# Turning the first eight attention units in four 64x64 tiles of TensorE, with diagonal blocks made by GpSimd

## The chip, the cores and the metric

The kernel runs on one core of one Trainium2 chip. The metric is the device time of one execution in microseconds. The core has five engines that run side by side, each through its own list of instructions in order: TensorE (PE in the profile; its weight loads are shown as PEld), VectorE (DVE), ScalarE (ACT), GpSimd (POOL), and SyncE (SP), which issues nearly all DMA transfers. They wait for each other through semaphores.

## What is computed

Two layers follow each other. The first is an attention in which only scores near the maximum of their row count; the second is a bilinear feed-forward layer. Cut from the reference:

```
q, k, v: (8, 8, 576, 64) float32; w_a, w_b: (512, 1536), w_out: (1536, 512) float64
scores = (q @ k^T) / sqrt(64)
thresh = max(scores, -1) - tau                       # tau = 0.02
attn   = exp(where(scores >= thresh, scores, -1e9) - max(scores, -1))
attn   = attn / (sum(attn, -1) + 1e-9)
x      = (attn @ v), heads side by side               # (4608, 512)
out    = ((x @ w_a) * (x @ w_b)) @ w_out              # (4608, 512) float32
```

## The kernel before

**Units.** Heads are taken in pairs (`i`, 32 of them), and the 576 query rows of a pair in blocks of 128 (`u`). A unit `(i, u)` is one such block for both heads of a pair, and the program is one long loop over the units (line 1062); I call one pass of it a slot. A unit goes through a pipeline that stretches over several slots, and PE's matmuls of the second layer are put between the steps of the first by `advance`, which counts matmul columns against a planned pace.

**The steps of a unit.** In slot `g`: `scores` (lines 389 to 413) makes the scores of both heads in PSUM (line 404) and takes the row maxima on DVE (line 411) and the thresholds (line 412). `weigh` (422 to 438) takes the exponential on ACT (lines 431 and 432), and on DVE masks it and sums the rows (line 435). `reciprocal` (440 to 449) makes `rcp`, one over each row's sum, on DVE. To multiply the weights by v, they have to be turned, so that the 576 keys lie on partitions. There are two ways for that:

- From the ninth unit on, `normalise` multiplies by `rcp` on ACT (line 454), and the blocks are turned on DVE (line 498) and through DRAM.
- The first eight units (`BY_PE = 8`: the first two blocks of the first four head pairs) are turned by PE. `diagonals` (456 to 463) makes, on ACT, a 128x128 identity times `rcp` for each of the two heads (line 462). In the next slot `turn_pe` (468 to 482) multiplies the weights by that diagonal: for each of nine groups of 64 keys and each head one matmul with 128 rows, 64 columns of weights and 128 moving columns (line 479). So the turn normalises as well. The results lie in two PSUM tiles: `tp` for the first eight groups, four to a bank, and `last` for the ninth. ACT copies `tp` to SBUF in two halves (line 481), DVE copies `last` (line 482).

One slot later still, `weighted_unit` (590 to 604) multiplies the turned weights by v (`product`, line 542: 36 matmuls in four 64x64 tiles of the array), `settle` copies the product out of PSUM (ACT line 549, DVE line 550), and `exchange` (line 565) copies halves across partitions on GpSimd. A float32 matmul stands in the trace as two records, each with a load of its own.

**Beside it: the weights of the second layer.** They are float64 in DRAM and are converted on the chip in 36 pieces of 128x512, two or three to a slot in the first slots. SP loads them (line 271, each tied to a PE instruction that was written before it, so that loads don't run ahead of the work). ACT takes the high and low words (lines 298 and 299), GpSimd clamps (line 305), DVE moves in the sign and shifts (lines 311 and 319), GpSimd adds (line 324). The order within a slot is written out in the loop: the remaining conversion steps of the pieces of the slot before are spread over it (`convert_rest`, lines 1092, 1146 and 1149), and the new pieces begin at lines 1138 and 1150. `diagonals` stands at line 1142: behind the clamp of the slot's first piece, ahead of the add of the earlier slot's second piece.

**PSUM** is handed out in four tiles of two banks (`banks`), shared by scores, turns, products and the second layer. Once a tile's reader is done, another takes it.

`make_identity` fills `ident` at line 350 on GpSimd. The diagonals lie in the space behind the turned q of the first four pairs (`first_sb`), in three places used in turn.

Of the kernel before, what the change touches and what calls it, by code (L numbers as in the profile page):

```python
# [13 lines left out]
AF = mybir.ActivationFunctionType  # L14
ALU = mybir.AluOpType
# [39 lines left out]
def kernel(  # L55
# [38 lines left out]
    nc = tc.nc  # L94
    B, H, S, D = q.shape
    P = 128
# [3 lines left out]
    HP = H // 2  # L100
    NT = 4
# [26 lines left out]
    def banks(n, name):  # L128

        return psum.tile([P, 2, 512], FP32, tag="banks", name=name)[:, :, 0:n]  # L130
# [95 lines left out]
    for f in range(NG):  # L226
        for c in range(HP):
            for dst, w in ((wa_sb, w_a), (wb_sb, w_b)):
                src = []
                for r in range(2):  # L230
                    chunks = [(2 * c + e) % HP * 2 + (r + (c >= HP // 2)) % 2 for e in range(2)]
                    cols = slice(f * CW + r * CH, f * CW + (r + 1) * CH)
                    rows = w[:, cols].bitcast(U32).rearrange("(k p) f -> p k f", p=D)
# [16 lines left out]
    first_sb = first_u32.bitcast(FP32)  # L250
# [97 lines left out]
    load_rows(3, "k", rooms[7])  # L348
    ident = more_sb[:, 2 * QUARTER:2 * QUARTER + P]
    make_identity(nc, ident)  # L350

# [14 lines left out]
    def prep_pe(i, name):  # L368

        m = loaded[i][name]  # L370
        if name == "q":
            mT = first_sb[:, i * S:(i + 1) * S]
        else:
            mT = work.tile([P, S], FP32, tag="kT", bufs=HP, name="kT")
        tp = banks(SH, "tp")
        for c in range(2):
            for n in range(NR // 2):
                nc.tensor.transpose(tp[:, c, n * R:(n + 1) * R], m[:, c * (NR // 2) + n], ident[0:R, 0:R])
        prepared.setdefault(i, {})[name] = mT
        return mT, tp  # L380
# [75 lines left out]
    def diagonals(i, u):  # L456

        ws, rcp = weights[i, u]
        g = units.index((i, u))
        dg = first_sb[:, HP * S + g % 3 * 2 * P:HP * S + (g % 3 + 1) * 2 * P].rearrange("p (j q) -> p j q", j=2)  # L460
        for j in range(2):
            nc.scalar.activation(dg[:, j], ident, AF.Copy, scale=rcp[:, j:j + 1])
        weights[i, u] = (ws, dg)

    def turned_tile():
        return work.tile([P, G + 1, NSLOT, Q], FP32, tag="wT", bufs=2, name="wT")

    def turn_pe(i, u):

        ws, dg = weights.pop((i, u))  # L470
        ws = [w.rearrange("p n e -> p (n e)") for w in ws]
        wT = turned_tile()[:, 0:G].rearrange("p g s e -> p (g s e)").rearrange("p (s w) -> p s w", w=P)
        turned[i, u, "pe"] = [wT[:, :, y * D:(y + 1) * D] for y in range(2)]
        tp = banks(512, "tp").rearrange("p y (s q) -> p y s q", s=NT)
        last = banks(P, "tp")
        for s in range(NSLOT):
            for j, w in enumerate(ws):
                to = (last[:, 0] if s == 2 * NT else tp[:, s // NT, s % NT])[j * D:(j + 1) * D]
                nc.tensor.matmul(to, w[:, s * D:(s + 1) * D], dg[:, j], start=True, stop=True)  # L479
        for y in range(2):  # L480
            nc.scalar.copy(wT[:, y * NT:(y + 1) * NT], tp[:, y])
        nc.vector.tensor_copy(wT[:, 2 * NT], last[:, 0])

    def parts(i, u):

# [553 lines left out]
    kT, tp = prep_pe(0, "k")  # L1039
# [22 lines left out]
    for g in range(len(units) + PV_LAG):  # L1062
# [49 lines left out]
        if 0 < g <= BY_PE:  # L1112
            turn_pe(*units[g - 1])
# [27 lines left out]
        if here and g < BY_PE:  # L1141
            diagonals(i, u)
        elif here:
            reciprocal(i, u, nc.scalar if converting else nc.vector)
            normalise(i, u)
# [80 lines left out]
```

## Time and profile before

| what | value |
|---|---|
| runs | 1420.72 us median of 3 (1419.43 to 1420.96) |
| profiled execution, first to last instruction (span) | 1417.0 us |
| median of the runs less that span | 3.7 us |
| mean granted clock of TensorE | 0.994 |
| busy over the span: PE / DVE / ACT / POOL | 1370.2 / 1013.7 / 679.9 / 495.7 us |
| records of line 479 (turn) | 288 matmuls, first at 19.0, last at 80.5 us, mean 0.30 us each as shown |
| records of line 462 (diagonals) | 16 on ACT, 0.41 us each as shown |
| line 481 / line 482 (copies of the turn) | 16 on ACT at 0.59 us / 8 on DVE at 0.27 us |
| PE idle before line 479 | 3.3 us "issue", 2.9 ACT, 0.6 ACT, 0.5 DVE (PE and PEld together) |
| busy in the stretch 0 to 100 us, line 479 on PE | 20.6 us |

The execution's own timed value is not given beside its profile, so its span stands for it. Matmuls are pipelined: the time shown for one is longer than the distance to the next, so a run of 36 records is measured from its first start to its last end. In the timeline one row merges neighbouring instructions of one line: start, length, engine, line, what it writes and reads, how many, and in brackets the idle time before it with what ended it.

### The profile page before, as it was taken

Reading aid. Unit: us, or ns where it says so; the run is one execution under the profiler, and the core shown is the slowest. Engines: PE = TensorE matmul, PEld = TensorE weight load, DVE = VectorE, ACT = ScalarE, POOL = GpSimd, SP = SyncE. Lnnn points to the kernel's source line nnn. Section 1 sums busy time; section 2 is a strip of 40 time slices with the busy share of each in tenths; the row PEclk is TensorE's granted clock in tenths of the full one; section 3 lists DMA queues with packets and bytes.
Section 4 is the critical chain, followed back from the end, with each engine's and each line's share of the span. In section 5 each row is a group of like instructions: output and inputs, shape, how many; then the busy total and the mean of one; then the engine's idle time right before and its main releaser. Section 6 shows DMA issues by size and latency. Waiting matters only on the chain.

```text
span 1417.0 us, 76257 instructions
## 1 busy us (share of the span) xinstructions
PE 1370.2 (97%) x33836; PEld 1229.6 (87%) x33836; DVE 1013.7 (72%) x2200; ACT 679.9 (48%) x1245; POOL 495.7 (35%) x678
## 2 busy tenths in 40 slices
PE   6788999999999999999999999999999999999998
PEld 5677579989878887979998999999888899799997
DVE  6898986778777877776767777677777776744424
ACT  5786554545445454545444545454545455431110
POOL 2674541606060606042333324150606060608100
PEclk9999999999999999999999999999999999999999
DMA  9967776667756775666555675567655775550000
GB/s 212 235 193 219 182 214 163 178 153 183 198 135 173 198 188 155 178 156 184 142 134 149 168 193 158 144 160 199 168 144 152 191 201 154 135 152 18 4 19 18
DMA packets 327000, 223.20 MB, mean 158 GB/s; under 512 B 171536, under 2 KB 310800, under 8 KB 326672
## 3 DMA queue, kind: packets, MB, share of 16 engines
q1 hardware_dynamic: 323712, 216.95, 59.2%
q8 instruction: 266, 4.36, 1.3%
q10 hardware_dynamic: 2960, 1.38, 0.4%
q14 instruction: 62, 0.51, 0.1%
HBM read 128.58 MB, written 89.65 MB: 154 GB/s over the span
## 4 chain that ended last, share of the span: by engine, by line
PE 86%; DVE 7%; DMA 3%; issue 2%; SPq 1%; ACT 0%; POOL 0%; DVEq 0%; POOLq 0%; ACTq 0%
PE pab L720 29%; PE po L885 20%; PE pab L824 16%; PE pv L542 10%; PE sc L404 10%; DVE mx L411 2%; DVE tw L498 2%; SPq L144 1%; DMA wT<-swap 1%; DVE tw L435 1%; PE tp L479 1%; DMA raw<-in_moe_w_a_dram 1%; DMA raw<-in_moe_w_b_dram 1%; DVE thr L412 0%; DVE u L790 0%
## 5 line engine op out<-in xcount | busy, mean ns | idle before, releaser
L411 DVE TENSOR_REDUCE mx<-sc 128x1 f32<-128x576 f32 x288 | 204.7, 752 | 125.8 <-PE sc L404 125.4
L454 ACT ACTIVATE tw<-tw,rcp 128x576 f32<-128x576 f32 x272 | 196.5, 770 | 202.3 <-DVE rcp L448 202.3
L682 POOL TENSOR_TENSOR h<-h,u 128x512 f32<-128x512 f32 x28 | 35.2, 1276 | 601.0 <-DVE h L794 426.1
L432 ACT ACTIVATE tw<-sc,bias,scalars 128x576 f32<-128x576 f32 x288 | 239.8, 833 | 10.9 <-PE pab L720 0.4
L435 DVE SCALAR_TENSOR_TENSOR tw<-sc,thr,tw 128x576 f32<-128x576 f32 x288 | 221.5, 799 | 10.4 <-ACT tw L432 9.9
L885 PE MATMUL po<-wo_sb,h 64*64 64x256 f32 x3264 | 205.8, 376 | 1.2 <-DVE h L794 1.1
L498 DVE STREAM_TRANSPOSE tw<-tw 128x576 f32<-128x576 f32 x272 | 194.4, 752 | 0.8 <-ACT tw L454 0.8
L885 PEld LDWEIGHTS po<-wo_sb,h 64*64 64x64 f32 x3264 | 157.0, 133 | 25.7 <-DVE h L794 2.6
L542 PE MATMUL pv<-wT,vm 64*64 64x160 f32 (+3 forms) x5184 | 169.2, 275 | 7.6 <-issue 3.6
L542 PEld LDWEIGHTS pv<-wT,vm 64*64 64x64 f32 x5184 | 157.4, 136 | 19.1 <-issue 9.8
L404 PE MATMUL sc<-kT,qT 64*64 64x288 f32 x2016 | 168.0, 404 | 1.1 <-DVE xt L550 0.5
L853 POOL TENSOR_TENSOR h<-h 128x256 f32<-128x256 f32 x168 | 117.4, 732 | 107.4 <-PE po L885 97.2
L885 PE MATMUL po<-sums_u,h 64*64 64x256 f32 x2448 | 153.4, 376 | 0.7 <-DVE h L832 0.7
L720 PE MATMUL pab<-xU,wb_sb 64*64 64x128 f32 x4352 | 138.0, 269 | 0.4 <-issue 0.3
L720 PEld LDWEIGHTS pab<-xU,wb_sb 64*64 64x64 f32 x4352 | 132.2, 133 | 3.7 <-issue 1.1
L885 PEld LDWEIGHTS po<-sums_u,h 64*64 64x64 f32 x2448 | 117.6, 133 | 19.4 <-DVE h L832 1.3
L404 PEld LDWEIGHTS sc<-kT,qT 64*64 64x64 f32 x2016 | 101.8, 133 | 22.6 <-issue 5.0
L549 ACT COPY xT<-pv 128x128 f32<-128x128 f32 (+1 forms) x68 | 17.7, 260 | 201.8 <-PE pv L542 200.2
L431 ACT ACTIVATE bias<-mx,scalars 128x1 f32<-128x1 f32 x288 | 83.1, 288 | 64.0 <-DVE mx L411 63.7
L550 DVE COPY xT<-pv 64x128 f32<-64x128 f32 (+1 forms) x136 | 38.1, 280 | 91.0 <-PE pv L542 89.7
L720 PE MATMUL pab<-xS,wa_sb 64*64 64x128 f32 x2176 | 101.8, 269 | 0.1
L531 ACT COPY kept<-po 128x512 f32<-128x512 f32 x65 | 34.8, 536 | 123.0 <-PE po L885 113.9
(156 smaller groups left out, 2414.3 us busy)
## 6 DMA issues: line engine op xcount, KB each, us to landing
wT<-swap SPq DMA_DIRECT2D x244, 288.0 KB, 3.9
swap<-tw SPq DMA_DIRECT2D x480, 144.0 KB, 2.9
vm<-in_v_dram SPq DMA_DIRECT2D x128, 72.0 KB, 2.5
swap<-tw SPq DMA_DIRECT2D x128, 72.0 KB, 3.0
kT<-in_k_dram SPq DMA_DIRECT2D x112, 72.0 KB, 3.3
wT<-swap SPq DMA_DIRECT2D x56, 144.0 KB, 3.3
out_dram<-kept SPq DMA_DIRECT2D x28, 256.0 KB, 3.9
qT<-in_q_dram SPq DMA_DIRECT2D x112, 40.0 KB, 2.8
```

The lines of the kernel that those rows point to most:

```text
L404: nc.tensor.matmul(sc[m][o * D:o * D + wide, c], qT[r, q0:q0 + wide], kT[r, c * SH:(c + 1) * SH], start=True, stop=True)
L411: nc.vector.tensor_reduce(mx[:, c], sc[j], axis=AX.XY, op=ALU.max)
L431: nc.scalar.activation(bias[:, j:j + 1], mx[:, j:j + 1], AF.Copy, scale=e_nscale)
L432: nc.scalar.activation(wb[j], sb[j], AF.Exp, bias=bias[:, j:j + 1], scale=e_scale)
L435: nc.vector.scalar_tensor_tensor(out=wv, in0=sb[j], scalar=thr[:, j:j + 1], in1=wv, op0=ALU.is_ge, op1=ALU.mult, accum_out=sums[:, j:j + 1])
L454: nc.scalar.activation(w, w, AF.Copy, scale=rcp[:, j:j + 1])
L498: nc.vector.transpose(w, w)
L542: nc.tensor.matmul(pv[c * D:(c + 1) * D, y], vm[rows, s], wT[y](rows, s), start=(s == 0), stop=(s == NSLOT - 1))
L720: nc.tensor.matmul(out[c * D:(c + 1) * D, r, f * P:(f + 1) * P], w[g][k][rows, w0:w0 + D], moving[k][rows], start=(fresh and k == 0 and f ...
L824: nc.tensor.matmul(pab[c:c + columns(), r], w[rows, f // n, k, fs + c:fs + c + columns()], moving, start=(k == 0), stop=(k == H - 1))
L853: (nc.vector if state["over"] else nc.gpsimd).tensor_tensor(*a, **kw)
L885: nc.tensor.matmul(po[c * D:(c + 1) * D, r, y], ht[rows, t0:t0 + D], other[rows, f], start=(f == 0), stop=(f == NF // 2 - 1))
```

## The change

The first eight units are turned in four tiles of 64x64 instead of two of 128x64. The 128 query rows of a unit fall in two halves of 64 (`r`). The diagonal matrix has nothing outside its two diagonal 64x64 blocks, so each half of the rows is multiplied only by its own block. Each matmul of 128 rows and 128 moving columns becomes two of 64 rows and 64 moving columns, and 18 matmuls to a turn become 36. Half `r` is written to bank `r` of the PSUM tile, so the copies to SBUF now take a half of the query rows each, with 64 of every 128 columns of the target.

The two diagonal blocks of both heads make a tile of 128x128 in place of two of 128x128. GpSimd makes it with one multiplication: `twice`, made once, holds the identity's two diagonal blocks on top of each other (64 columns), and is multiplied with `rcp` along the columns. ACT makes no diagonals any more. Order, tiles in PSUM, and everything behind the eighth unit's turn stay.

```diff
     make_identity(nc, ident)
+    twice = first_sb[:, HP * S + 3 * P:HP * S + 3 * P + D]
+    nc.gpsimd.tensor_tensor(twice, ident[:, 0:D], ident[:, D:P], op=ALU.add)
...
         ws, rcp = weights[i, u]
         g = units.index((i, u))
-        dg = first_sb[:, HP * S + g % 3 * 2 * P:HP * S + (g % 3 + 1) * 2 * P].rearrange("p (j q) -> p j q", j=2)
-        for j in range(2):
-            nc.scalar.activation(dg[:, j], ident, AF.Copy, scale=rcp[:, j:j + 1])
+        dg = first_sb[:, HP * S + g % 3 * P:HP * S + (g % 3 + 1) * P].rearrange("p (j q) -> p j q", j=2)
+        nc.gpsimd.tensor_tensor(dg, twice.unsqueeze(1).to_broadcast([P, 2, D]), rcp.unsqueeze(2).to_broadcast([P, 2, D]), op=ALU.mult)
         weights[i, u] = (ws, dg)
...
-        tp = banks(512, "tp").rearrange("p y (s q) -> p y s q", s=NT)
-        last = banks(P, "tp")
+        tp = banks(512, "tp").rearrange("p y (s q) -> p y s q", q=D)
+        last = banks(D, "tp")
         for s in range(NSLOT):
-            for j, w in enumerate(ws):
-                to = (last[:, 0] if s == 2 * NT else tp[:, s // NT, s % NT])[j * D:(j + 1) * D]
-                nc.tensor.matmul(to, w[:, s * D:(s + 1) * D], dg[:, j], start=True, stop=True)
-        for y in range(2):
-            nc.scalar.copy(wT[:, y * NT:(y + 1) * NT], tp[:, y])
-        nc.vector.tensor_copy(wT[:, 2 * NT], last[:, 0])
+            for r in range(2):
+                rows = slice(r * D, (r + 1) * D)
+                for j, w in enumerate(ws):
+                    to = (last[:, r] if s == 2 * NT else tp[:, r, s])[j * D:(j + 1) * D]
+                    nc.tensor.matmul(to, w[rows, s * D:(s + 1) * D], dg[rows, j], start=True, stop=True)
+        for r in range(2):
+            nc.scalar.copy(wT[:, 0:2 * NT, r * D:(r + 1) * D], tp[:, r])
+        nc.vector.tensor_copy(wT[:, 2 * NT].rearrange("p (r q) -> p r q", r=2), last)
```

## The prediction

> **What bounds the kernel now.** I read the head of the page first, because it says in which part of the span the change lies. The 288 matmul records of line 479, which are all that `turn_pe` issues, lie between 19.0 and 80.8 us of a span of 1417.0 us. So only the first 6% is touched, and what is gained or lost there has to be carried through to the end.
>
> ```profile
> span 1417.0 us, 76257 instructions
> ...
> PE   6788999999999999999999999999999999999998
> ...
> DMA  9967776667756775666555675567655775550000
> ...
> q8 instruction: 266, 4.36, 1.3%
> ```
>
> Each digit is a slice of 35.4 us. From the fifth slice on PE is busy nine tenths or more: whatever time PE has won or lost by then stays. In the first two slices it is only at six and seven tenths, so something else sets the pace there. The busy times by stretch name the candidate:
>
> ```profile
> core 0: us, PE busy (x) PEld busy (x) DVE busy (x) ACT busy (x) POOL busy (x), PEclk, DMA share, GB/s
> ...
> 20.00:44.00 24.00, 18.52 (x396) 15.16 (x392) 22.61 (x55) 20.29 (x44) 14.21 (x19) 1.00 1.17 223
> 44.00:70.00 26.00, 20.21 (x402) 17.57 (x403) 22.25 (x49) 19.36 (x40) 18.58 (x21) 0.93 1.05 237
> 70.00:100.00 30.00, 26.89 (x498) 24.10 (x499) 28.08 (x59) 26.23 (x53) 21.79 (x25) 0.94 0.66 187
> ```
>
> VectorE (DVE) is busy 22.61 of 24, 22.25 of 26 and 28.08 of 30 us, more than any other engine. In its timeline the row maxima of one step of the loop ("slot") follow those of the last at 25.34, 33.29, 39.90, 46.93, 56.82, 67.00, 77.71, 86.33 and 96.46 us, and between 33.3 and 77.7 it idles only 0.21, 0.47, 0.75, 0.93, 1.43 and 1.00 us: **4.8 us**. All six fall at or behind 49 us and wait for PE. So a faster PE can gain about 4.8 us here and no more, as long as DVE's own work stays.
>
> Why PE is late there, its timeline shows. The last bracket is the idle time before a row:
>
> ```profile
> 56.82 1.28 PE L542 MATMUL pv<-wT,vm 64*64 64x64 f32 x72
> 59.52 1.93 PE L479 MATMUL tp<-first_u,tw 128*64 128x128 f32 x31 [1.42 <-ACT tw L432]
> 62.58 0.54 PE L479 MATMUL tp<-first_u,tw 128*64 128x128 f32 x5 [1.13 <-issue]
> ...
> 70.09 0.34 PE L542 MATMUL pv<-wT,vm 64*64 64x64 f32 x6 [1.83 <-issue]
> 70.36 3.23 PE L479 MATMUL tp<-first_u,tw 128*64 128x128 f32 x36
> ```
>
> Two things are to be seen: the turn takes 2.2 to 3.2 us where 72 matmuls of 64x64 take 1.28, and PE waits for "issue", that is for nothing that the view can name. There are four such waits: 0.56 us until 47.29, 0.56 until 54.66, 1.13 until 62.58 and 1.83 until 70.09. I held them against the packets of queue q8 in the trace. Queue q8 carries 266 packets (4.36 MB) for PE's 67,672 matmuls and loads: 254 instructions to a packet. Its packets end at 45.72, 53.17, 61.09 and 68.63 us, and PE goes on 1.57, 1.49, 1.49 and 1.46 us later, each time exactly 256 instructions after the last stop. **PE waits there for its own instructions.** A packet starts 4.6 to 5.2 us after PE has entered the block before it, while the DMA share is over 1, and 1.1 to 1.9 us after it once the share has fallen to 0.66: about 7.5 us from block to block in the first case and 4.4 in the second.
>
> **The change part by part.** (1) *Turns on PE.* Now: 36 records a turn, 2.71, 2.19, 2.19, 2.48, 3.02, 2.47, 3.23 and 2.47 us, 20.8 in all. Afterwards: 9 slots x 2 halves x 2 heads x 2 records = 72 records of 64 columns through 64x64 tiles, the form of line 542's matmuls, hence 1.28 us each, 10.2 in all. Bounds: 1.2 us from the pv's own start-to-start, and 2.6 (no gain) from line 479 itself if the four tiles don't overlap. I take 1.28: PE loses **10.5 us** of work, of which only DVE's idle time can become time: **-4.8 us** at best. Zero is the other end. Were DVE not the cover, the whole 10.5 would count.
>
> (2) *Instructions for PE.* A turn has 72 loads and matmuls now and 144 after. A slot without the second layer goes from 232 to 304, one with three groups of 16 matmuls of line 824 from 328 to 400. At 7.5 us for 256 instructions, 400 would need 11.7 us where slots last 7 to 10.7. Moving the stops (every 256 instructions from the 449th) along the longer stream puts them in the pv of the fourth slot, the pv of the fifth, and the turn of the sixth, with waits of about 2.1, 3.2 and 4.2 us, and one of 0.8 in the eighth: 10.3 against 4.1 now. I let the packet's delay shrink as PE falls back, since line 271's loads are tied to PE's progress (SP's waits name PE sc, tp and pab): a PE that is late by d us shortens the delay by d. Of the 10.3, DVE feels 1.5 (its copies of pv in the fifth slot), 0.3, 0.6 and 0.5 us: an estimate of **+2.9 us** in place of the 4.8 that vanish. Bounds: 0 if the fetch keeps pace, and +8.8 if the delay never shrinks.
>
> (3) *Diagonals on GpSimd (POOL).* Gone from ACT: 16 of line 462, 0.35 us apart, 5.6 us. ACT's next work (conversions) is not late today, nothing waits for it, so 0. Added on POOL: 8 multiplications of 128x128. There is no row of that size; lines 682 (512 columns, 1.28 us) and 853 (256 columns, 0.73 us) give 2.1 ns a column and 0.46 us; bounds 0.31 (one copy of line 565) and 0.73. POOL has room (14.21 of 24 us). The new wait for `rcp` holds back the clamp and add queued behind it; that add waits for a DVE shift later than `rcp` anyway. `dg` is needed a slot later, behind scores and pv (some 3 us), so it is never late. `twice` falls into POOL's idle stretch until 14.07 us.
>
> But POOL's work holds up DVE:
>
> ```profile
> 34.75 0.23 DVE L412 TENSOR_SCALAR thr<-mx,scalars 128x2 f32<-128x2 f32 x1
> ...
> 41.34 0.60 DVE L412 TENSOR_SCALAR thr<-mx,scalars 128x2 f32<-128x2 f32 x1
> ```
> ```profile
> 41.31 0.61 POOL L305 TENSOR_SCALAR wb_sb<-wb_sb 128x512 f32<-128x512 f32 x1
> ```
>
> The same two columns take DVE 0.23 us alone and 0.60 when POOL has begun just before; lines 311 and 319 stretch likewise (0.68 to 1.10, 0.42 to 1.50). The Trainium skill, "SBUF — State Buffer", section "Who interferes with whom", has the rule: the shared port pair is locked for a whole instruction, and DVE operations in a two-port mode or with two SBUF inputs wait for GpSimd. The rows agree. The new multiplication begins with `rcp`, and line 311 comes 0.2 us behind `rcp`: I take 0.35 us in six of the slots, **+2.1 us**; bounds 0 and 8 x 0.73 = 5.8.
>
> (4) *Copies.* Line 481 and line 482 move as many elements as before; ACT's first copy today starts only with the eighth slot block done, so it doesn't matter that the halves are now split otherwise. 0.
>
> **Sum**: -4.8 + 2.9 + 2.1 = +0.2 us at 78 us. From there DVE has no idle time until 98, and then PE takes over, so I carry it 1:1. The profiled span, 1417.0, becomes 1417.2; the runs' median lies 3.7 us above the span, which I leave: 1420.72 + 0.2, rounded to **1421**.
>
> **The rivals.** *Forecast: the three terms cancel*, 1418 to 1424: chance 0.40. For it: each is read from rows; against: all three are estimates of a few us.
>
> *The fetch keeps pace* (0.27): -4.8 with 0 to 2.1 of the lock, 1416 to 1418. For it: from 70 us on no stop at a block lasts, though pv runs at full rate. Against: four stops before that. The Trainium skill, "Runtime: NRT & Kernel Launch", section "Instruction fetch mechanics", says that fetching is hidden behind issue; by that rule the sum would be -2.7 and the time 1418.0. The trace disagrees before 70 us, with the four waits above.
>
> *PE is fed too slowly* (0.20, the slower side). If the delay stays at 5 us for as long as the DMA queues are full, each 256 instructions take 7.5 us up to 66 us, and the scores of the ninth slot come some 4 us late instead of early: with part of the lock, 1425. It decides once PE crosses 256 instructions in under 7.5 us. For it: SP's loads also wait for earlier transfers, so the queues may stay full whatever PE does. Against: SP is tied to PE's progress.
>
> *The lock costs more* (0.10): each multiplication blocks DVE for all of 0.73 us, 5.8 - 1.9 = +3.9, 1424.6. *The four tiles don't overlap* (0.03): the turn stays at 2.6 us with twice the instructions, about 1427.
>
> **How the numbers follow.** Differences of 0.2% (2.8 us) and more can be told from none in this kernel. Faster than 1417.9: most of the second case and a little of the first, 0.25. Slower than 1423.6: the third to fifth cases and a little of the first, 0.34. Within: 0.41. The range takes in the second case with the full 4.8 and some of PE's other gain, and the slow cases at their prices: 1414 to 1428.
>
> **What would show it.** Line 479: 72 records in 1.3 us per turn. PE's waits for "issue" before 100 us: 10 us instead of 4.1 (the second case: 4 or less). Lines 311 and 319 of DVE longer by 2 us in sum, starting with POOL's new operation. Row maxima of the ninth slot at 77.7 +- 2 us, and everything after that moved by the same amount. I am wrong if DVE is not the bound, when the ninth slot would begin 6 us or more earlier, or if PE's stops lie elsewhere.

## The result, and the profile after

The changed kernel takes 1432.1 us (median of 4 runs, 1427.4 to 1433.8) beside 1420.8 us for the kernel before on the same chip: ratio **1.0078, interval 1.0049 to 1.0107**. It is slower by about 11 us. The prediction, 1421 with a range to 1428, was wrong.

The page of the changed kernel, the lines that answer to those shown of before (line numbers behind the change are 2 or 3 higher: the scores are line 406, the row maxima 413, the turn 482, the product by v 545, the second layer 827):

```profile
span 1429.4 us, 76827 instructions
...
PE   6778999999999999999999999999999999999998
...
DMA  9967786567756675666545676567655775550000
...
q8 instruction: 269, 4.41, 1.3%
```

The span is 12.4 us longer; three more packets of instructions were fetched (576 / 256 = 2.25). PE's third slice, 71 to 107 us, lost a tenth, and the other digits ahead of it are the same, so the page alone doesn't show where the loss begins. Busy times by stretch, in the columns explained above (PE, PEld, DVE, ACT, POOL, each with its count, then granted clock, DMA share, GB/s):

```profile
20.00:44.00 24.00, 16.72 (x473) 13.25 (x469) 20.88 (x51) 15.20 (x31) 14.43 (x19) 0.82 1.16 222
44.00:70.00 26.00, 18.89 (x439) 16.38 (x431) 18.42 (x47) 17.84 (x36) 16.72 (x21) 0.74 0.90 214
70.00:100.00 30.00, 22.46 (x574) 20.25 (x574) 28.36 (x58) 23.16 (x46) 22.30 (x28) 0.94 0.57 161
```

Two columns matter. DVE is busy 18.42 us of the second stretch, where it was 22.25: it waits. And the granted clock of PE, 1.00 and 0.93 in the first two stretches before, is **0.82 and 0.74**. The trace's record of the clock knows only two values, full and half. Between 11 and 70 us it was half for 13.7 us from 14.8 on and for 13.7 us from 48.9 on; before, from the 20th microsecond on, for 3.4 us from 47.4 on.

PE's timeline at the second of these half-clock stretches, and the next slot behind it:

```profile
46.22 1.58 PE L406 MATMUL sc<-kT,first_u 64*128 64x288 f32 x6 [1.39 <-DVE tw L437]
49.40 1.32 PE L406 MATMUL sc<-kT,first_u 64*128 64x288 f32 x2 [1.60 <-issue]
50.65 2.20 PE L545 MATMUL pv<-wT,vm 64*64 64x64 f32 x72
52.62 1.70 PE L482 MATMUL tp<-first_u,tw 64*64 64x64 f32 x53
56.77 0.91 PE L482 MATMUL tp<-first_u,tw 64*64 64x64 f32 x19 [2.44 <-issue]
57.60 2.08 PE L827 MATMUL pab<-xT,wa_sb 64*128 64x128 f32 x16
...
62.74 1.24 PE L406 MATMUL sc<-kT,first_u 64*128 64x288 f32 x8
...
68.31 1.16 PE L827 MATMUL pab<-xS,wb_sb 64*128 64x128 f32 x16
...
71.09 1.24 PE L406 MATMUL sc<-kT,first_u 64*128 64x288 f32 x8
```

The scores stop for instructions in mid-unit and go on at half clock. The product by v takes 2.20 us where it takes 1.28 at full clock, a group of the second layer 2.08 where it takes 1.16. The second stop, in the turn, 256 instructions after the first, falls into the same half-clock stretch. Behind it the three groups of the second layer take 5.1 us up to the next scores (57.60 to 62.74), where the three of the slot after take 2.8 at full clock (68.31 to 71.09).

The first half-clock stretch begins before the change does: at 14.8 us, where the first 64x64 turn starts at 18.81. It already slows the third slot's scores, here before and after:

```profile
24.09 1.25 PE L404 MATMUL sc<-kT,first_u 64*128 64x288 f32 x8 [1.37 <-DVE kT L383]
```
```profile
23.99 2.30 PE L406 MATMUL sc<-kT,first_u 64*128 64x288 f32 x8 [0.94 <-DVE kT L385]
```

DVE's waits on PE from 20 to 100 us (total, times, longest), in which the next scores' lateness is the largest:

```profile
DVE mx L413 <- PE sc L406: 7.8, 5, 3.6
DVE xT L553 <- PE pv L545: 1.6, 2, 1.1
DVE wT L485 <- PE tp L482: 1.2, 1, 1.2
```

So the seventh slot begins at 63.91 us instead of 56.82, and the ninth at 82.45 instead of 77.71. Behind the ninth the distance to before stays at 5 to 7 us up to the 25th slot (214.9 against 208.3) and grows to 12.4 at the end.

### The profile page after: what moved, and what is told of

It is laid out like the page before. It is cut to its first block, busy times and chain, and to the rows that moved or that the text cites. A ratio compares the mean times of both kernels' runs of the same rounds, so it can differ in the third digit from the quotient of the medians.

```text
span 1429.4 us, 76827 instructions
## 1 busy us (share of the span) xinstructions
PE 1370.9 (96%) x34124; PEld 1211.0 (85%) x34124; DVE 1013.6 (71%) x2200; ACT 673.8 (47%) x1229; POOL 500.1 (35%) x687
## 4 chain that ended last, share of the span: by engine, by line
PE 85%; DVE 7%; DMA 4%; issue 2%; SPq 2%; ACT 0%; POOL 0%; POOLq 0%; DVEq 0%
PE pab L723 28%; PE po L888 20%; PE pab L827 16%; PE sc L406 10%; PE pv L545 10%; DVE mx L413 2%; DVE tw L501 2%; DVE tw L437 1%; DMA wT<-swap 1%; DMA vm<-in_v_dram 1%; DVE thr L414 1%; SPq L271 1%; SPq L144 1%; DMA swap<-tw 1%; SPq L198 1%
## 5 line engine op out<-in xcount | busy, mean ns | idle before, releaser
L434 ACT ACTIVATE tw<-sc,bias,scalars 128x576 f32<-128x576 f32 x288 | 239.6, 832 | 10.3 <-DMA wT<-swap 0.4
L888 PEld LDWEIGHTS po<-wo_sb,h 64*64 64x64 f32 x3264 | 151.1, 133 | 33.3 <-DVE h L797 2.6
L888 PEld LDWEIGHTS po<-sums_u,h 64*64 64x64 f32 x2448 | 112.1, 133 | 26.0 <-DVE h L835 1.5
```

The costliest lines, as they stand in the source:

```text
L434: nc.scalar.activation(wb[j], sb[j], AF.Exp, bias=bias[:, j:j + 1], scale=e_scale)
L888: nc.tensor.matmul(po[c * D:(c + 1) * D, r, y], ht[rows, t0:t0 + D], other[rows, f], start=(f == 0), stop=(f == NF // 2 - 1))
```

## The experiments

**Theory**: PE's instruction stream became longer (144 instead of 72 loads and matmuls a turn) at the time when full DMA queues hold back its packets; PE waits for instructions, and the idle time halves its clock for a multiple of 3.4 us. No run takes load off the queues, so that part of the theory is argued from the traces and not tested. **Rivals**: the port lock between GpSimd and DVE; PE's clock falling because PE has less work, instructions or not; something in the 64x64 turn itself; and, for what grows behind 200 us, the new place of the instruction blocks. All ratios are to runs of the kernel before on the same chip, beside the run in question. On the chips of the experiments that kernel lay at 1424 to 1427.5 us and spread over 11 to 16 us, so only ratios are compared; most intervals are about ±0.2%.

**pool_only**: the turn of before, diagonals by GpSimd.

```diff
-        for j in range(2):
-            nc.scalar.activation(dg[:, j], ident, AF.Copy, scale=rcp[:, j:j + 1])
+        nc.gpsimd.tensor_tensor(dg, ident.unsqueeze(1).to_broadcast([P, 2, P]), rcp.unsqueeze(2).to_broadcast([P, 2, P]), op=ALU.mult)
```

> The turn of before (128x64 tiles, 18 matmuls), only the diagonals moved from ACT to one GpSimd multiplication of 128x256 a unit. Theory (too many PE instructions for the fetch, then PE's clock halved while it waits): nothing changes on PE, so 1419 to 1422, with no more half-clock time than before. Rival (the shared port lock between GpSimd and DVE makes the loss): a larger GpSimd operation than in the change, so 1426 or more, with lines 311 and 319 of DVE longer by several us in sum.

**tiles_act**: the turn of the change, diagonals by ACT.

```diff
-        nc.gpsimd.tensor_tensor(dg, twice.unsqueeze(1).to_broadcast([P, 2, D]), rcp.unsqueeze(2).to_broadcast([P, 2, D]), op=ALU.mult)
+        for j in range(2):
+            nc.scalar.activation(dg[:, j], twice, AF.Copy, scale=rcp[:, j:j + 1])
```

> The 64x64 turn of the change, with the diagonals made by ACT again (two of 128x64 a unit). Theory: all of the loss stays, 1428 to 1434, with waits for issue of some 8 us before 100 us and half-clock stretches of 10 us and more. Rival (port lock): 1418 to 1421.

Measured: pool_only **1.0005 (0.9987 to 1.0023)**, tiles_act **1.0050 (1.0032 to 1.0068)**. The GpSimd half of the change costs nothing that can be measured, although pool_only's operation is twice as wide; the loss comes with the tiles. The port lock falls as the cause of a loss of this size; 2 or 3 us of it would still fit in pool_only's interval.

**more_instr**: the kernel before, with matmuls of 16 columns added to the turns, so that a turn has the change's number of instructions and no less work.

```diff
+                nc.tensor.matmul(to[:, 0:16], w[:, s * D:(s + 1) * D], dg[:, j, 0:16], start=True, stop=True)
                 nc.tensor.matmul(to, w[:, s * D:(s + 1) * D], dg[:, j], start=True, stop=True)
```

> The kernel before with 18 more small matmuls (16 columns, overwritten at once by the real ones) in each of the eight turns, so that a turn has the 144 loads and matmuls of the change, but none of its saving. Theory: PE's waits for issue before 100 us rise from 4 to 8 us or more, and the time to 1427 or more. Rival (PE's clock falls because the change gives PE less work, not because it waits for instructions): PE has more work here, so no additional half-clock time, and at most 1 us for each of the three or four turns on the path, 1420 to 1424.

Measured 1.0042 (1.0027 to 1.0056), with the old turn. To tell instructions from added work, the same line only for some of the units: **b_more_late** (the last three turns, `if units.index((i, u)) >= 5`) and **b_more_early** (the first five, `< 5`).

> The kernel before with the 18 small matmuls of more_instr only in the last three of the eight turns (slots 7 to 9, where the DMA queues are no longer full). Theory (instructions cost where their fetch waits in full DMA queues): 0.999 to 1.002. Rival (the small matmuls cost as work, about a us for a turn on PE's path, and these are the turns on it): 1.002 or more, no less than the five early ones.

> The kernel before with the small matmuls of more_instr only in the first five of the eight turns (slots 2 to 6). Theory (instructions cost while the DMA queues are full): the loss of more_instr, 1.003 to 1.006, with the step from the sixth to the seventh slot at 13 us or more instead of 10. Rival (number of instructions plays no part; more_instr lost by work on the path): 0.999 to 1.002, as the three late ones.

Measured: late **0.9996 (0.9980 to 1.0012)**, early **1.0078 (1.0053 to 1.0102)**. The late turns bear the same addition for nothing that shows, although it isn't hidden there (in b_more_late's profile DVE waits 2.0 us for one of these turns); in the early ones, while the DMA share is 0.9 or more, it costs as much as the change. The five early turns alone even cost more than all eight in more_instr, whose interval theirs hardly meets; why isn't known. The timeline of b_more_early shows the stop in the fifth slot:

```profile
40.89 0.57 PE L544 MATMUL pv<-wT,vm 64*64 64x64 f32 x23
43.51 1.14 PE L544 MATMUL pv<-wT,vm 64*64 64x64 f32 x49 [2.04 <-issue]
```

The changed kernel stops at the very same matmul, 23 into the product, at 41.5 us. The step from the sixth slot to the seventh, which I expected at 13 us, is 10.6 here; its sixth slot was already late, at 50.5 us.

**late_tiles** and **early_tiles**: the change itself only for the last three, or only for the first five of the eight units, the others as before; late_tiles was run twice (late_tiles2). In these the diagonals lie in two places used in turn, not three.

```diff
+        if g >= 5:      # early_tiles: g < 5
             ...         # diagonals and turn of the change
+        else:
             ...         # diagonals and turn of before
```

> Only the last three of the eight turns (slots 7 to 9) are made as in the change; the first five as before (ACT diagonals, 128x64 tiles). Theory (PE's instructions come too slowly while the DMA queues are full, up to about 66 us, and its clock halves): these turns lie behind that stage, ratio 0.998 to 1.001. Rival (each 64x64 turn costs something by itself, by its mode, lock or shorter work): three eighths of the loss, 1.002 to 1.003.

> Only the first five turns (slots 2 to 6) as in the change. Theory: all of the loss, 1.004 to 1.007. Rival (each turn costs something by itself): five eighths, about 1.003.

> late_tiles once more, to narrow its interval: the turns that PE has instructions for gain the wait of DVE that they remove, 1 to 2 us: 0.998 to 1.000.

Measured: late **0.9986 (0.9967 to 1.0006)** and 1.0007 (0.9988 to 1.0026), early **1.0054 (1.0031 to 1.0078)**; the whole change beside the first late_tiles and early_tiles, **after_again**, 1.0059 (1.0037 to 1.0080).

> The changed kernel once more, beside the runs of this call. Ratio to before 1.003 to 1.010; its first 100 us show half-clock stretches of 10 us and more. With a_fill192 (1.0051) it says whether the later place of the block boundaries cost anything: 1.008 or more if it did, 1.003 to 1.006 if not.

So the 64x64 turn is no loss in the last three units, and its first five uses carry all of the loss. In late_tiles it is as quick as the prediction said: the eight groups in 1.1 us, then a wait for the PSUM tile of the ninth, which DVE has to give back:

```profile
67.52 1.11 PE L489 MATMUL tp<-first_u,tw 64*64 64x64 f32 x64
68.86 0.34 PE L489 MATMUL tp<-first_u,tw 64*64 64x64 f32 x8 [0.23 <-DVE xT L570]
```

It gains nothing that shows: no version of these was clearly faster than the kernel before.

**a_lesspv** and **b_lesspv**: both kernels with the first eight units' product by v over 5 of the 9 key groups (4 of 9 of that sum is left out), 64 instructions a unit fewer.

```diff
-    def product(wT, vm, n):
+    def product(wT, vm, n, NSLOT=NSLOT):
...
-        pv = product([lambda rows, s, t=t: t[rows, s] for t in wT], loaded[i]["v"], P)
+        pv = product([lambda rows, s, t=t: t[rows, s] for t in wT], loaded[i]["v"], P, 5)
```

> The changed kernel with the product by v of the first eight units taken over 5 of the 9 groups of keys (leaves out 4 of 9 of that sum): 64 instructions a unit fewer for PE, so that a slot has about as many as before, and still less matmul work than the change. Theory (number of instructions): the loss is gone, ratio 0.996 to 1.001. Rival (PE has too little work, so its clock falls): as slow as the change or slower, 1.005 and more.

> The kernel before with the product by v of the first eight units over 5 of 9 groups (leaves out the rest): 64 instructions a unit fewer, no change to the turn. Theory: the waits for issue before 75 us, 5 us before, fall to 1 or less, ratio 0.996 to 0.999, unless the clock falls for want of work: then 0.999 to 1.002. Rival (instructions are no bound): only 0.5 us a unit of PE work saved, under DVE's cover, 0.999 to 1.001.

Measured: a_lesspv 1.0028 (1.0006 to 1.0050), b_lesspv 1.0015 (0.9998 to 1.0033). With that many instructions fewer the change costs about half of what it did (the intervals overlap), and not nothing as I expected: its profile still has a stop of 2.0 us and is at half clock for 22 us between 28 and 70 us. So the number of instructions alone doesn't explain the loss, nor does the clock alone. b_lesspv gains nothing, although its profile shows no stop; before_again, below, shows that the kernel before has none either in some executions.

**warm** and **a_lesspv_warm**: the change and a_lesspv with long matmuls (unused results) behind three of the early turns. They are written into the tile of the ninth group, which is wider for it.

```diff
-        last = banks(D, "tp")
+        full = banks(512, "tp")
+        last = full[:, :, 0:D]
...
+        if 2 <= units.index((i, u)) < 5:
+            for n in range(2):
+                for j in range(2):
+                    nc.tensor.matmul(full[j * D:(j + 1) * D, 0, D:512], ident[:, 0:D], ws[j][:, 0:512 - D], start=True, stop=True)
```

> The changed kernel with four long matmuls (448 columns, results unused) behind the turns of the third to fifth unit: some 2 us more work for PE in slots 4 to 6, with only 16 more instructions a turn. It keeps PE busy where it waits for VectorE. Theory (the loss is the waits for instructions and, about as much, the half clock that follows on idle time): less half-clock time between 45 and 65 us, ratio 1.001 to 1.004. If the clock alone makes the loss: 1.000. Rival (the clock plays no part, the waits alone): added work on the path, 1.006 to 1.008.

> a_lesspv (product by v over 5 of 9 groups of keys, leaves out the rest) with the same long matmuls: few instructions and enough work. Theory: both causes are taken away, ratio 0.997 to 1.001. Rival (something else in the 64x64 turn): as a_lesspv, 1.003 or more.

Measured: 1.0131 (1.0098 to 1.0164) and 1.0070 (1.0046 to 1.0095). Both miss: the added work made them slower. In warm's profile the half-clock time between 45 and 65 us did fall, from 13.7 to 3.4 us, and the seventh slot began at 61.7 us, 2.2 earlier than in the change; but DVE's copy of the ninth group waits for the added matmuls, which write the same tile (2.2 us in this profile). That profile is one of the quicker executions (1437 of 1434 to 1447 us), and what the slower ones lose is not known. How much of the loss is the clock's alone therefore stays open.

**a_fill192, b_shift64, b_shift112, b_shift256**: 48, 16, 28 and 64 small matmuls ahead of one later unit's scores (the 21st, or the 17th), which shift all block boundaries behind. In a_fill192 (the changed kernel) they come back to where they were before; in b_shift64 (the kernel before) they go to where the change puts them.

```diff
+        if units.index((i, u)) == 16:
+            for n in range(16):
+                e, o = n % 2, n // 2 % 2
+                r = slice(e * D, (e + 1) * D)
+                nc.tensor.matmul(sc[e][o * D:(o + 1) * D, 0, 0:16], qT[r, 0:D], kT[r, 0:16], start=True, stop=True)
```

> The changed kernel with 48 small matmuls (16 columns, overwritten by the scores) put ahead of the 21st unit's scores: 192 more loads and matmuls, so that with the change's 576 the later program is shifted by 768, three whole blocks of 256. Theory (the later half of the loss is PE's waits at block boundaries, which the shift moved to worse places): waits at block boundaries after 200 us fall from about 10 us to about 4, and the time by 4 to 6 us, to 1426 to 1428. Rival (the later loss is not from the place of the boundaries): 1432 to 1434, the added work itself being 1 to 2 us.

> The kernel before with 16 small matmuls (64 instructions) ahead of the 17th unit's scores: the block boundaries of everything behind lie where the change puts them (576 = 2 x 256 + 64), the first eight units are untouched. If the later half of the loss comes from the place of the boundaries: 1.003 to 1.005. If not: 1.000 to 1.002, as b_shift256.

> The same with 28 small matmuls (112 instructions), about where early_tiles and warm put the boundaries, whose profiles had the longest waits behind 100 us. Place of boundaries: 1.004 or more. If not: 1.000 to 1.002.

> The same with 64 small matmuls (256 instructions): boundaries as before, so it shows what the added matmuls cost by themselves, some 1 to 3 us: 1.000 to 1.002 in either theory.

Measured: a_fill192 1.0051 (1.0034 to 1.0068), as tiles_act beside it; b_shift64 1.0030 (1.0009 to 1.0051), b_shift112 1.0041 (1.0018 to 1.0065), control b_shift256 1.0023 (1.0003 to 1.0042). So 64 small matmuls cost some 0.2% by themselves. Moving the boundaries costs 0.07% and 0.18% over that, with intervals that overlap, and a gain of a_fill192 of the size of what its own 48 matmuls cost wouldn't show. PE's waits do follow the place: behind 100 us its waits for "issue" sum to 2.7 to 7.3 us in the six profiles whose later boundaries lie as in the kernel before (before, before_again, pool_only, b_lesspv, b_shift256, a_fill192), and to 7.3 to 14.3 us in the other fourteen. But late_tiles, with 9.3 and 8.8 us of them, isn't slower: that the place of the blocks costs time is not shown.

**before_again**, for the spread:

> The kernel before once more, for its profile on the chip of the experiments and for the spread of the comparison: ratio 0.998 to 1.002, ninth slot at 77 to 80 us; waits at block boundaries behind 100 us of 9 to 15 us as in the other profiles of this chip, if they belong to the chip and not to the change.

Measured 0.9997 (0.9977 to 1.0017). Its profile has no stop for instructions between 20 and 100 us at all and 6.8 us of half clock between 28 and 70 us, and the ninth slot begins at 76.4 us; PE's waits for "issue" behind 100 us, which I expected at 9 to 15 us, are 2.7:

```profile
44.00:70.00 26.00, 22.64 (x438) 20.01 (x440) 24.30 (x53) 20.91 (x45) 19.14 (x23) 0.87 0.97 232
```

So the four stops that I read in the first profile come and go from execution to execution, and cost this kernel little. Over all profiles: the ninth slot begins at 74.0 to 77.7 us in the five whose first 16 units are those of before, and at 80.7 to 84.7 us in the seven with more instructions in the early turns and nothing left out or filled in (the change twice, tiles_act, a_fill192, early_tiles, more_instr, b_more_early); means 75.5 and 82.9, **7.4 us** apart. That is most of the 8.4 us that after_again's ratio makes of 1427.5 us. The split is not quite clean: pool_only, which isn't slower, has its ninth slot at 79.7 us. From the 25th slot to the end the profiles take 1209 to 1214 us (before, before_again, pool_only) and 1214 to 1229 us (the seven); late_tiles and b_more_late, which are not slower, lie at 1214 to 1217. Whether some us are lost there as well stays open: one execution of each can't settle it.

The same profiles show that part of the loss comes ahead of every stop. The fourth slot begins at 33.5 us in the mean of the five. In the change, after_again, tiles_act, a_fill192 and early_tiles, which have the 64x64 turn from the first unit on, it begins 0.9 to 3.6 us later, of the 6.4 to 9.2 us by which their ninth slot is late, and PE hasn't waited for instructions since 20 us; each has 3.4 to 13.7 us at half clock before it. In more_instr and b_more_early, with the old turn, it begins 0.3 and 0.7 us later. So the change loses something at half clock ahead of any stop, which more_instr and b_more_early hardly do. That PE's smaller amount of work lowers the clock there is likely, but no run tests it by itself.

## Why the prediction was wrong, point by point

*DVE sets the pace up to 98 us, PE's gain is at most its 4.8 us of idle time*: right for the kernel before. b_lesspv and late_tiles, which free PE, gain nothing measurable. But the 4.8 us belong to one execution: in before_again DVE idles 1.2 us between the same slots.

*(1) The turn*: right in size. 72 records take 1.11 + 0.34 us at full clock (late_tiles; 1.28 predicted), 2.2 at half.

*(2) Instructions for PE*: the step that failed, in what DVE feels of PE's waits. The prediction put these waits at 10.3 us before 100 us and let DVE feel +2.9 us of them in place of 4.8. PE's waits for instructions came to 1.35 + 1.60 + 2.44 = **5.4 us**, half of that. The packets' delay did shrink: to 3.4 to 4.8 us in the five blocks that PE enters between 29 and 57 us, from 4.2 to 5.2 us in the same five before. Two stops lie where the prediction put them (product in the fifth slot, turn of the sixth); the product of the fourth slot has none, and the scores of the sixth have one that was not foreseen. Yet DVE's waiting from the fourth slot to the ninth is 1.16 + 1.13 + 1.22 + 3.62 = **7.1 us**, more than the 4.8 that it replaces, and the scores of the fourth slot already come 1.6 us late, because PE runs at half clock from 14.8 to 28.5 us. Together with 0.8 us more of DVE's own time these make the 4.7 us at the ninth slot (1.6 + 7.1 - 4.8 + 0.8). What was missing is the clock: I read 0.93 in the stretch of before and gave the halving no term at all. The Trainium skill, "TensorE: Matmul & The Clock Gate", section "What's actually happening", has it: a monitor looks at PE's activity in windows of 3.4 us and grants full or half clock. The traces agree: but for the last one of a run, which the end of the record cuts, each half-clock stretch lasts 3.4, 6.8, 10.2 or 13.7 us. Of the longest wait, 3.62 us for the seventh slot's scores, about 2.4 are the half clock, by an estimate from the rows above (5.1 us for three groups of the second layer instead of 2.8). Over all runs, how the loss divides between waiting and clock was not separated (warm). The start of the first half-clock stretch isn't the change's doing: before_again is at half clock from 15.3 us too, but for 6.8 us instead of 13.7, and its fourth slot begins at 33.8 us (33.3 in the first profile, 34.9 in the change).

*(3) The lock between GpSimd and DVE, +2.1 us*: not seen, and not excluded. The operation takes 0.40 us alone and 0.56 as the median (0.46 predicted), and DVE and it do meet:

```profile
40.63 0.84 POOL L463 TENSOR_TENSOR first_u<-first_u,rcp 128x128 f32<-128x128 f32 x1
```
```profile
41.13 0.62 DVE L319 TENSOR_SCALAR wb_sb<-wb_sb 128x512 uint32<-128x512 uint32 x1
```

The operation takes 0.84 us instead of 0.40 here, the shift 0.62 instead of 0.42. But the 2 us more that lines 311 and 319 were to show aren't there: a piece's two shifts take 1.35 us in the first 100 us, before and after. All that DVE's own time grew by up to the ninth slot is the 0.8 us above. The runs can't tell +2.1 us (0.15%) from none: pool_only, at twice the width, lies at +0.05% ± 0.18%.

*(4) Copies, ACT: nothing*: nothing speaks against it; tiles_act and the change, which differ in ACT's work, lie at 1.0050 and 1.0059.

*The sum, carried 1:1*: +0.2 us was forecast at the ninth slot, and 4.7 came. From the 9th to the 25th slot the distance went from 4.7 to 6.6 us; to the end it doubled, of which the part behind the 25th slot is within what single executions differ by.

*The rivals*: "PE is fed too slowly" had the right sign, and for the ninth slot nearly the right size (some 4 us late, 4.7 measured). Its price for the whole (+4 us) is less than half of what was measured, the clock isn't in it, and I gave it 0.20. Its rule, "once PE crosses 256 instructions in under 7.5 us", doesn't hold for every execution: in before_again PE crosses two blocks in 6.2 and 5.8 us before 70 us and stops behind neither, since the packets start 1.2 to 3.9 us after PE has entered the block before. "The fetch keeps pace" fell for the change, with its 5.4 us of waits, and with it, for this stage, the rule cited there that fetching is hidden.

## What to carry to other kernels

Count instructions as well as time when matmuls are cut into smaller tiles: a turn that takes half as long with twice as many loads and matmuls needs its instructions at four times the rate, and in a stage like this one (DMA share about 1, 256 instructions in 6.6 to 7.4 us between PE's stops) that rate can be the bound. Less work and short waits can also cost the clock, as in the scores at 49.40 us, which go on at half clock; so judge a gain on PE first by what else paces that stage (here DVE, with 4.8 us to give) and then by the granted clock of the stretch.

## What the runs showed of the hardware that I had not expected

PE's clock fell although no single wait was long: in the changed kernel at 48.9 us, with PE busy for 1.6 us of the 3.4 us before that and no idle stretch in them above 1.1 us. The fetch of a packet of 256 instructions takes 0.9 to 1.4 us once it starts (first 110 us of the first profiles of both kernels). When it starts varies more than the DMA share tells: with the share between 1.0 and 1.2 it started 4.2 to 5.2 us after PE had entered the block before in the first profile of the kernel before, and 1.2 to 3.9 us after it in before_again. The same program had stops of 4.1 us in sum between 20 and 100 us in the one execution, and none in the other.
